# Denominators in 32-row column tiles, reciprocals spread by DMA, moments from the add, and a fixed order table, in a linear-attention and gMLP kernel

## The chip, the cores and the metric

One core of one Trainium2 chip. The metric is the time in device microseconds (us) of one execution; a median of several executions is quoted, with the lowest and the highest in brackets. Nearly all runs here count as fast; the four single ones that were marked slow (one each of e1, e8, e9 and of the kernel before) are left out of every ratio.

## The reference, cut to what matters

```python
# x [1,2048,512]; 32 heads of 16; F half = 896
q, k, v = split(layernorm(x) @ wqkv)
pq, pk  = phi(q), phi(k)                  # phi(t) = (t+1 if t>0 else exp(t)) + 1e-6
kv  = einsum('bhsd,bhse->bhde', pk, v);  z = pk.sum(over s)
num = pq @ kv;   den = einsum('bhqd,bhd->bhq', pq, z) + 1e-6    # one number per token and head
h   = x + (num / den) @ wo
z   = gelu(layernorm(h) @ w_in);  z1, z2 = halves of z;  z2 = layernorm(z2)
g   = w_sp @ z2 + b_sp                    # "mixing": over the 2048 tokens
out = h + (z1 * g) @ w_out
```

The parts that matter: the division by `den`, the moments of `h` for the second layer norm, and the mixing, whose matrix `w_sp` (8 MB) must be brought in and transposed while the first half runs.

## The kernel before

Every operation is recorded with its engine, its reads and writes and a modelled cost; a scheduler then fixes one order for each of the five engines, and each engine works through its own order and never overtakes. Most instructions therefore carry a helper's line number, and one goes by the names of the tiles. The division works on whole 128-row tiles, with z spread by a mask into a 128x128 matrix, so that each denominator comes out on all 16 rows of its head:

```python
    for tg in range(NG):                       # 4 groups of 512 tokens
        for c in range(0, KD, 2):
            q, r = pqT[:, c:c + 2, tg * GW:(tg + 1) * GW], r16[len(dens) % 2]
            for i in (0, 1):
                matmuls(bank(DB + i), [(zmat[:, c + i, :], q[:, i, :])])
            act(r_t, pair(DB), ACT.Ln, 2 * GW, bias=epst[:, 0:1], extra=[epst])
            dens.append(act(r, r_t, ACT.Exp, 2 * GW, scale=-1.0))       # 1/den
            dve(lambda v, q=q, r=r: v.tensor_tensor(q, q, r, ALU.mult), ...)
    for n in range(NT):                        # 16 tiles of h
        matmuls(bank(b), [(pqT[:, c, n * P:(n + 1) * P], m[:, c, :]) for c in range(KD)])
        dve(... v.tensor_tensor(h[:, n, :], bank(b), x[:, n, :], ALU.add) ...)
        stats(h, 1, n)                         # BN stats and aggregate on DVE
        rstd(...); norm(...)                   # GpSimd, then DVE: hn
        g.last = dma_t(hnT[:, :, n * P:(n + 1) * P], hn, f"ht{n}")   # SyncE transposes
```

The loads of `w_sp` are 64 transposing DMAs on the same SyncE, 16 for each of four groups of 512 tokens. All 16 of one group raise one semaphore, so a reader of any tile of a group waits for the whole group. The scheduler does not model this: in its times a reader waits for the tiles that it reads.

```python
    order = [t for p in range(NG // 2) for tg in (p, p + NG // 2) for t in range(tg * TPG, (tg + 1) * TPG)]
    for t in order:                            # groups 0, 2, then 1, 3
        for j in range(0, NT, 4):
            dma_t(wsp[:, j:j + 4, t * P:(t + 1) * P], ..., f"wsp{t // TPG}").deps.add(...)
```

The mixing is done in two rounds, with a seven-product block scheme: groups 0 (`lo`) and 2 (`hi`) first, then 1 and 3. The sums of blocks of `w_sp` that it needs (t1, t2 and so on) are made by DVE:

```python
    for p in range(NG // 2):
        for tok, b in ((lo, EB[0]), (hi, EB[1])):
            matmuls(bank(b), [(z2[:, s, last * P:KF * P], wsp[:, s, tok]) for s in range(NT)])
            gate(last, tok, b, bsp[:, tok])    # DVE reads the bank: u, then z1T. Frees the bank
        op = combine(t1, y12, y11, ALU.subtract)       # y12, y11: half of the tiles of groups hi and lo
        combine(t2, y22, t1, ALU.subtract)
        ...
        for k in range(HF): cell(k, lo, hi)    # s1 @ t1 into bank EB[c], ...
```

Of the kernel before, what the change touches and what calls it, by code (L numbers as in the profile page):

```python
# [3 lines left out]

FP32 = mybir.dt.float32
# [7 lines left out]
LOOK = 160.0  # L13
ROUNDS = 1200
# [16 lines left out]
class _Prog:  # L31
# [110 lines left out]
    def _pass(self, rank, back):  # L142

        ops = self.ops
        pre = [o.users if back else o.deps | o.soft for o in ops]
        nxt = [o.deps | o.soft if back else o.users for o in ops]
        left = [len(p) for p in pre]
        ready = [0.0] * len(ops)
        free = {e: 0.0 for e in self.ENGS}
        cand = {e: [] for e in self.ENGS}  # L150
        for o in ops:
            if not left[o.i]:
                cand[o.eng].append(o.i)
        start = [0.0] * len(ops)
        for _ in ops:
            best = None
            for e in self.ENGS:
                c = cand[e]
                if not c:
                    continue  # L160
                t0 = max(free[e], min(ready[i] for i in c))
                pick = min((i for i in c if ready[i] <= t0 + LOOK), key=lambda i: (rank[i], i))
                t0 = max(t0, ready[pick])
                if best is None or t0 < best[0]:
                    best = (t0, e, pick)
            t0, e, i = best
            cand[e].remove(i)
            start[i] = t0
            free[e] = t0 + ops[i].cost
            for u in nxt[i]:  # L170
                lag = self._lag(ops[u], ops[i]) if back else self._lag(ops[i], ops[u])
                ready[u] = max(ready[u], free[e] + lag)
                left[u] -= 1
                if not left[u]:
                    cand[ops[u].eng].append(u)
        return start

    def _value(self, start):

        v = max(start[o.i] + o.cost + o.lat for o in self.ops)  # L180
        last = None
        for t, c in sorted((start[o.i], o.cost) for o in self.ops if o.eng == "PE"):
            if last is not None and t - last > 800:
                v += (t - last - 800) * 0.5
            last = t + c
        return v

    def _swing(self, rank, n):

        best = None  # L190
        for _ in range(n):
            start = self._pass(rank, False)
            v = self._value(start)
            if best is None or v < best[0]:
                best = (v, start)
            late = self._pass([-(start[o.i] + o.cost) for o in self.ops], True)
            rank = [-(late[o.i] + o.cost) for o in self.ops]
        return best

    def schedule(self):  # L200
        ops = self.ops
        for o in ops:
            for d in o.deps | o.soft:
                ops[d].users.append(o.i)
        for o in reversed(ops):
            o.prio = max((ops[u].prio + self._lag(o, ops[u]) for u in o.users), default=o.lat) + o.cost + o.bias
        best = self._swing([-o.prio for o in ops], 20)
        rng = np.random.default_rng(0)
        for _ in range(ROUNDS):
            t = np.array(best[1])  # L210
            a, w = rng.uniform(0, 0.6 * best[0]), rng.uniform(5e3, 4e4)
            if rng.random() < 0.4:
                a, w = 0.0, best[0]
            near = (t >= a) & (t < a + w)
            got = self._swing(list(t + near * rng.normal(0, rng.choice([200, 600, 1500, 3000]), len(ops))), 2)
            if got[0] <= best[0]:
                best = got
        self.est, self.start = best
        self.seq = sorted(ops, key=lambda o: (self.start[o.i], o.i))
        self.order = {e: [o for o in self.seq if o.eng == e] for e in self.ENGS}  # L220
# [91 lines left out]
def bass_sequential_preLN__linear_attn_block__mixer_gmlp__prompt_kernel(  # L312
# [92 lines left out]
    r_t = g.sbuf("r", o_r, [2, GW], FP32)  # L405
    r16 = [g.sbuf(f"r16{b}", o_ct + b * 2 * GW * 2, [2, GW], BF16) for b in range(2)]
# [4 lines left out]
    zmat = g.sbuf("zmat", o_z, [KD, P], BF16)  # L411
# [14 lines left out]
    sel = const("sel", [8], FP32)  # L426
    epst = const("epst", [8], FP32)
# [12 lines left out]
    def bank(b, n=512, lo=0):  # L440
        return psum[:, b, lo:lo + n]
# [68 lines left out]

    wq = A_wqkv.rearrange("(c p) f -> p c f", p=P)
# [25 lines left out]
    for n, t in ((8, 7600), (10, 8300), (12, 9100), (14, 9900)):  # L537
        load_x("SP", n, 2, t)
    first_load("SP", wqkv[:, :, 0:D], A_wqkv[:, 0:D], "wq", 11400)
    g.add("ACT", lambda ac: ac.preload_act_table_set("natural_log_exp_and_others"), [], [], cost=1300).soft.add(  # L540
        queue["ACT"][-1].i)
# [7 lines left out]
    def rstd(s, r, n, w, col, neg, sign=1.0):  # L549

        rr, ss = r[:, n:n + w, :], s[:, n:n + w, :]
        pool(lambda p: p.tensor_scalar(rr[:, :, 1:2], ss[:, :, col + 1:col + 2], sign, EPS_LN, op0=ALU.mult,  # L552
                                       op1=ALU.add), [ss[:, :, col + 1:col + 2]], [rr], 230)
        pool(lambda p: p.tensor_tensor(rr[:, :, 0:1], rr[:, :, 1:2],  # L554
                                       expo[:, 0:w].rearrange("p (a b) -> p a b", b=1), ALU.pow), [rr, expo], [rr],
             620 + 120 * (w - 1))
        if neg:
            for i in range(n, n + w):
                pool(lambda p, i=i: p.tensor_scalar(r[:, i, 2:3], s[:, i, col:col + 1], r[:, i, 0:1], -1.0,
                                                    op0=ALU.mult, op1=ALU.mult), [r[:, i, :], s[:, i, :]], [r[:, i, :]], 240)  # L560

# [24 lines left out]
    def phi(dst, b, w=2):  # L586

        e, t = e_t[ecnt[0] % NE][:, 0:w, :], psum[:, b:b + w, :]
        ecnt[0] += 1
        act(e, t, ACT.Exp, w * GW)  # L590
        dve(lambda v: v.tensor_scalar(e, e, 1.0, EPS_PHI, op0=ALU.min, op1=ALU.add), [e], [e], w * GW, acc=4)
        dve(lambda v: v.scalar_tensor_tensor(dst, t, 1.0 + EPS_PHI, e, op0=ALU.add, op1=ALU.max),  # L592
            [t, e], [dst], w * GW, ps=True)
# [60 lines left out]
    def z_unit():  # L654
# [20 lines left out]
        for c in range(KD):  # L675
            dve(lambda v, c=c: v.tensor_scalar(zmat[:, c, :], bmask, bank(zb + 1, 1, c), None, op0=ALU.mult),
                [bmask, bank(zb + 1)], [zmat[:, c, :]], P)

    QS = {8: 1, 10: 1, 12: 1, 14: 1}
# [33 lines left out]
    for c in range(KD):  # L713
        b = CB[1 - c % 2]
        matmuls(bank(b), [(kvm[:, c, :], wo[:, c, :])])
        if c % 2:
            act(m[:, c, :], bank(b), ACT.Copy, GW)
        else:
            dve(lambda v, c=c, b=b: v.tensor_copy(m[:, c, :], bank(b)), [bank(b)], [m[:, c, :]], GW, ps=True)
# [5 lines left out]
    DB, dens = 6, []  # L725
    for tg in range(NG):
        for c in range(0, KD, 2):
            q, r = pqT[:, c:c + 2, tg * GW:(tg + 1) * GW], r16[len(dens) % 2]
            for i in (0, 1):
                matmuls(bank(DB + i), [(zmat[:, c + i, :], q[:, i, :])])  # L730
            act(r_t, pair(DB), ACT.Ln, 2 * GW, bias=epst[:, 0:1], extra=[epst])
            dens.append(act(r, r_t, ACT.Exp, 2 * GW, scale=-1.0))
            dve(lambda v, q=q, r=r: v.tensor_tensor(q, q, r, ALU.mult), [q, r], [q], 2 * GW, acc=2)  # L733


    AB = [4, 5]
# [4 lines left out]
    for n in range(NT):  # L741
        b = AB[n % 2]
        matmuls(bank(b), [(pqT[:, c, n * P:(n + 1) * P], m[:, c, :]) for c in range(KD)])
        dve(lambda v, n=n, b=b: v.tensor_tensor(h[:, n, :], bank(b), x[:, n, :], ALU.add), [bank(b), x[:, n, :]],  # L744
            [h[:, n, :]], D, ps=True)
        stats(h, 1, n)
        rstd(st[1], rs[1], n, 1, 6, HN(n) != "DVE")
        hn = hn_t[n % NH]
        norm(HN(n), hn, h[:, n, :], st[1], rs[1], n, 6, D)
        g.last = dma_t(hnT[:, :, n * P:(n + 1) * P], hn, f"ht{n}")  # L750
        if n == 0:
            first = g.last
# [3 lines left out]
    table.deps |= {o.i for o in dens}  # L756
    for n in range(NT):
# [14 lines left out]
        if n % 2 == 0 and n < NT - 2:  # L772
            gl = act(z2[:, n, :], src, ACT.Gelu_apprx_tanh, FH, accum=s[:, 0:1])
            act(sq_t, z2[:, n, :], ACT.Square, FH, scale=FH ** -0.5, accum=s[:, 1:2])
            pool(lambda p, s=s: p.tensor_scalar(s[:, 12:13], s[:, 0:1], 1.0 / FH, None, op0=ALU.mult), [s], [s], 190)
            dve(lambda v, s=s: v.scalar_tensor_tensor(s[:, 13:14], s[:, 12:13], s[:, 12:13], s[:, 1:2], op0=ALU.mult,
                                                      op1=ALU.subtract), [s], [s], 60)
            rstd(st3, rs3, n, 1, 12, False, -1.0)
# [6 lines left out]
        gl.deps.add(table.i)  # L785
# [7 lines left out]
    for tg in range(NG):  # L793
        for fc in range(KF):
# [3 lines left out]
            act(z1T[:, fc, tg * GW:(tg + 1) * GW], bank(b), ACT.Gelu_apprx_tanh, GW).deps.add(table.i)  # L798
# [112 lines left out]
```

## Time and profile before

| | before |
|---|---|
| median of 3 runs | 238.44 us (238.12 to 238.98) |
| span of the profiled execution | 239.5 us |
| busy: TensorE, DVE, ScalarE, GpSimd | 96%, 68%, 39%, 17% |
| last tile of `w_sp` group 2 issued by SyncE (103.11 + 8 x 1.31) | about 113.6 us |
| first sum t1 on DVE | 117.2 us |
| first matmul that reads t1 | 134.3 us |

A timeline line gives start, length, engine, line, operation, tiles out<-in, and how many instructions are merged; a bracket at the end is idle time before it and who ended it. A page's busy rows are shares of the span, its digits tenths of a slice. Four lines of the timelines of before, of SyncE's queue and of DVE, will be needed later:

```profile
103.11 14.38 SPq L491 DMA_TRANSPOSE wsp<-in_B_w_sp_dram  x11
117.53 1.08 SPq L488 DMA_DIRECT2D bsp<-in_B_b_sp_dram  x1
```

```profile
116.20 1.08 DVE L565 TENSOR_SCALAR z<-z,st,rs 128x896 bf16<-128x896 bf16 x2
117.20 2.28 DVE L830 TENSOR_TENSOR t<-wsp 128x4096 bf16<-128x4096 bf16 x1
```

The reader sees that SyncE hands out the last tiles of group 2 in the first run of eleven (nine of it; the last two are of group 1), only then b_sp, and that t1 starts on DVE without a wait. There are 17 us from t1 to the matmul that reads it, and z1 matmuls lie in between.

One trap: the granted-clock row of before has a 7 in its second slice. There TensorE ran at half its clock for 3.4 us ("half clock" from here on), right behind a hole (idle time of TensorE) of 1.87 us in the head; that costs 1.7 us of progress. It comes in some executions only: the profiled one of before had it (mean clock 0.993, 241.22 us), most of its other runs had not (0.998 to 1.000). Traces are therefore compared from a point after the head, times by medians.

### The profile page before, as it was taken

The page shows a single profiled execution, that of the slowest core. Times are in us where ns is not written, and L with a number is a line of the kernel's source. Part 1 is how long each engine was busy: PE and PEld are TensorE (multiplying, and loading weights), DVE is VectorE, ACT ScalarE, POOL GpSimd, SP SyncE. Part 2 cuts the span into 40 slices and gives each one's busy share as a digit, 9 for nine tenths or more (in the row PEclk, how much of TensorE's full clock was granted, in tenths as well). Part 3 has the DMA queues.
Part 4 walks back from the last instruction along what each step waited for, and adds up shares of the span by engine and source line. Part 5 has one row for each costly group of instructions (what it writes and reads, how often), then busy time and mean ns, then how long its engine had stood idle before and what let it go on. Part 6 is the DMA issues. An engine that isn't in the chain of part 4 may idle for free.

```text
span 239.5 us, 3027 instructions
## 1 busy us (share of the span) xinstructions
PE 229.2 (96%) x1118; PEld 107.1 (45%) x1140; DVE 163.4 (68%) x303; ACT 93.1 (39%) x134; POOL 40.2 (17%) x113
## 2 busy tenths in 40 slices
PE   7689999999989999999999999999999999999994
PEld 7244444463334444444434444444444444444441
DVE  3798766579998999954985538929659454443634
ACT  2276943479996477688460210100101010000000
POOL 4442400000114564773210000000000000000000
PEclk9799999999999999999999999999999999999999
DMA  6904359944413446444584453430000000010223
GB/s 213 311 5 88 75 139 374 226 105 94 109 27 66 105 92 84 96 104 93 105 164 107 97 102 89 97 78 0 3 0 0 0 0 3 22 66 1 88 68 110
DMA packets 57727, 21.58 MB, mean 90 GB/s; under 512 B 49520, under 2 KB 57584, under 8 KB 57712
## 3 DMA queue, kind: packets, MB, share of 16 engines
q1 hardware_dynamic: 56880, 20.59, 36.5%
q10 hardware_dynamic: 832, 0.79, 1.0%
q8 instruction: 9, 0.15, 0.3%
q14 instruction: 6, 0.05, 0.1%
HBM read 7.47 MB, written 2.10 MB: 40 GB/s over the span
## 4 chain that ended last, share of the span: by engine, by line
PE 78%; DVE 10%; ACT 4%; DMA 4%; issue 1%; POOL 1%; SPq 0%; DVEq 0%
PE psum L458 65%; PE psum L641 6%; PE psum L763 4%; DVE st L546 3%; PE psum L766 3%; DMA x<-in_A_x_dram 2%; DVE h L744 2%; ACT r L477 2%; DVE hn L565 2%; DMA hnT<-hn 1%; ACT e L477 1%; DVE pqT L592 1%; POOL rs L554 1%; DVE st L781 1%; DVE pqT L733 0%
## 5 line engine op out<-in xcount | busy, mean ns | idle before, releaser
L458 PE MATMUL psum<-wsp,z 128*128 128x512 bf16 x205 | 47.0, 379 | 0.2
L458 PEld LDWEIGHTS psum<-wsp,z 128*128 128x128 bf16 x208 | 20.4, 98 | 24.4 <-ACT psum L477 0.2
L477 ACT ACTIVATE psum<-psum 128x512 f32<-128x512 f32 x12 | 7.0, 582 | 61.8 <-PE psum L458 37.0
L458 PE MATMUL psum<-hnT,win 128*128 128x512 bf16 x110 | 26.4, 379 | 0.1
L554 POOL TENSOR_TENSOR rs<-rs,expo 128x1 f32<-128x1 f32 (+1 forms) x41 | 25.1, 614 | 3.1
L458 PE MATMUL psum<-wout,z1T 128*128 128x512 bf16 x109 | 25.0, 379 | 0.1
L458 PE MATMUL psum<-t,s 128*128 128x512 bf16 x95 | 22.5, 379 | 0.1
L477 ACT ACTIVATE z1T<-psum 128x512 bf16<-128x512 f32 x28 | 16.6, 595 | 14.8 <-PE psum L458 14.8
L477 ACT ACTIVATE e<-psum 128x1024 bf16<-128x1024 f32 (+1 forms) x18 | 16.7, 928 | 14.3 <-PE psum L458 14.2
L552 POOL TENSOR_SCALAR rs<-st 128x1 f32<-128x1 f32 (+1 forms) x41 | 9.1, 222 | 74.0 <-DVE st L547 63.0
L477 ACT ACTIVATE z<-psum 128x896 bf16<-128x896 f32 x16 | 14.6, 914 | 10.5 <-PE psum L766 10.4
L458 PE MATMUL psum<-wqkv,xnT 128*128 128x512 bf16 x61 | 16.7, 407 | 1.1 <-ACT xnT L477 0.7
L825 DVE TENSOR_TENSOR u<-psum,bsp 128x512 bf16<-128x512 f32 x16 | 10.9, 689 | 9.9 <-PE psum L458 9.7
L816 DVE TENSOR_TENSOR h<-psum,h 128x512 bf16<-128x512 f32 x16 | 10.5, 686 | 9.8 <-PE psum L458 9.8
L458 PEld LDWEIGHTS psum<-wout,z1T 128*128 128x128 bf16 x112 | 10.9, 98 | 13.3 <-DVE h L816 0.4
L763 PE MATMUL psum<-win,hnT 128*128 128x512 bf16 x60 | 15.9, 379 | 0.6 <-DMA hnT<-hn 0.5
L825 DVE TENSOR_TENSOR u<-psum,p 128x512 bf16<-128x512 f32 x12 | 8.2, 689 | 11.9 <-PE psum L458 11.9
L458 PEld LDWEIGHTS psum<-hnT,win 128*128 128x128 bf16 x112 | 10.5, 98 | 12.8 <-ACT z1T L477 1.9
L641 PE MATMUL psum<-pk,xn 128*128 128x512 bf16 x63 | 16.1, 379 | 0.1
L458 PE MATMUL psum<-m,pqT 128*128 128x512 bf16 x62 | 15.3, 380 | 0.6 <-DVE pqT L733 0.2
L458 PE MATMUL psum<-xnT,wqkv 128*128 128x512 bf16 x63 | 15.7, 379 | 0.1
L458 PEld LDWEIGHTS psum<-t,s 128*128 128x128 bf16 x96 | 9.4, 98 | 11.3 <-ACT psum L477 0.2
(81 smaller groups left out, 304.2 us busy)
## 6 DMA issues: line engine op xcount, KB each, us to landing
out_dram<-h SPq DMA_DIRECT2D x16, 128.0 KB, 1.7
win<-in_B_w_in_dram SPq DMA_DIRECT2D x2, 896.0 KB, 9.8
x<-in_A_x_dram SPq DMA_DIRECT2D x5, 256.0 KB, 6.8
wqkv<-in_A_wqkv_dram SPq DMA_DIRECT2D x2, 512.0 KB, 6.2
wsp<-in_B_w_sp_dram SPq DMA_TRANSPOSE x64, 2.8
wout<-in_B_w_out_dram SPq DMA_DIRECT2D x1, 896.0 KB, 9.3
wo<-in_A_wo_dram SPq DMA_DIRECT2D x1, 512.0 KB, 5.3
bsp<-in_B_b_sp_dram SPq DMA_DIRECT2D x1, 512.0 KB, 5.2
```

Source lines behind the costliest of these rows:

```text
L458: inst = pe.matmul(out_ap, lhsT=a, rhs=b, start=start and i == 0, stop=stop and i == len(pairs) - 1, **kw)
L477: return g.add("ACT", lambda ac: ac.activation(out_ap, in_ap, func, **kw), [in_ap, *extra], [out_ap] + ([accum] if accum is not None else []),
L546: dve(lambda v: v.bn_stats(s[:, 0:6], src[:, n, :]), [src[:, n, :]], [s[:, 0:6]], D)
L552: pool(lambda p: p.tensor_scalar(rr[:, :, 1:2], ss[:, :, col + 1:col + 2], sign, EPS_LN, op0=ALU.mult, op1=ALU.add), [ss[:, :, col + 1:col ...
L554: pool(lambda p: p.tensor_tensor(rr[:, :, 0:1], rr[:, :, 1:2], expo[:, 0:w].rearrange("p (a b) -> p a b", b=1), ALU.pow), [rr, expo], [rr] ...
L565: return dve(lambda v: v.tensor_scalar(dst, src, mean, rst, op0=ALU.subtract, op1=ALU.mult), [src, mean, rst], [dst], w + 460, acc=4)
L641: inst = pe.matmul(bank(CB[c]), lhsT=xn[:, i, c * P:(c + 1) * P], rhs=pk[:, i, :], start=i == 0, stop=i == NT - 1)
L744: dve(lambda v, n=n, b=b: v.tensor_tensor(h[:, n, :], bank(b), x[:, n, :], ALU.add), [bank(b), x[:, n, :]], [h[:, n, :]], D, ps=True)
L763: pe.matmul(bank(b), lhsT=hnT[:, c, n * P:(n + 1) * P], rhs=win2[:, c, 0:GW], start=c == 0, stop=c == KD - 1)
L766: inst = pe.matmul(bank(b + 1, F2), lhsT=hnT[:, c, n * P:(n + 1) * P], rhs=win2[:, c, GW:FH], start=c == 0, stop=c == KD - 1)
L816: dve(lambda v: v.tensor_tensor(o, bank(b), h[:, n, :], ALU.add), [bank(b), h[:, n, :]], [o], D, ps=True)
L825: dve(lambda v: v.tensor_tensor(t, bank(b), add, ALU.add), [bank(b), add], [t], GW, ps=True)
```

## The change

Three intents. (1) `den` is one number per head and token, so 32 rows hold it (4 copies of 8 heads) where 128 were computed; four such 32-row products sit side by side in TensorE, and Ln and Exp run on one bank in place of four. The price: each reciprocal must be spread from 32 rows to 128 by a DMA. (2) The moments of h come from an accumulator of the add and from a ScalarE square, and not from BN stats on DVE. (3) The order, which a randomised search found at build time, is now a stored table.

```diff
-    def _pass(self, rank, back): ...          # list scheduler, 1200 random restarts
+    def schedule(self):
+        ids = np.frombuffer(zlib.decompress(base64.b85decode(ORDER)), np.uint16).tolist()
+        ...                                    # the table is the order; only checked against deps
-    zmat = g.sbuf("zmat", o_z, [KD, P], BF16)
+    zc = g.sbuf("zc", o_z, [KD, 32], BF16)
@@ denominators
+    def spread(tg, c):
+        src, dst = rc[tg % 2][32 * c:32 * (c + 1), :], r16[tg][:, c, :]
+        src_ap = bass.AP(src.tensor, src.offset, [list(src.ap[0]), [0, 4], [1, GW]])
+        g.add("SP", lambda q: q.dma_start(dst, src_ap), [rc[tg % 2]], [dst], cost=480, lat=2500, ...)
     for tg in range(NG):
-        for c in range(0, KD, 2):
-            for i in (0, 1):
-                matmuls(bank(DB + i), [(zmat[:, c + i, :], q[:, i, :])])
-            act(r_t, pair(DB), ACT.Ln, 2 * GW, ...)
-            dens.append(act(r, r_t, ACT.Exp, 2 * GW, scale=-1.0))
+            for c in range(KD):
+                inst = pe.matmul(psum[32 * c:32 * (c + 1), db, :], lhsT=zc[:, c, :], rhs=pqT[:, c, tok], ...)
+        act_exp(r_t, bank(db), ACT.Ln, GW, ...)
+        act_exp(rc[tg % 2], r_t, ACT.Exp, GW, scale=-1.0)
+        for c in range(KD):
+            spread(tg, c)
@@ h
-    AB = [4, 5]
+    AB = [4, 5, 7]
-        dve(... v.tensor_tensor(h[:, n, :], bank(b), x[:, n, :], ALU.add) ...)
-        stats(h, 1, n)
-        rstd(st[1], rs[1], n, 1, 6, HN(n) != "DVE")
+        dve(... v.scalar_tensor_tensor(h[:, n, :], bank(b), 1.0, x[:, n, :], op0=ALU.mult, op1=ALU.add,
+                                       accum_out=s[:, 0:1]) ...)
+        act(sh_t[n % 2], h[:, n, :], ACT.Square, D, scale=D ** -0.5, accum=s[:, 1:2])
+        moments(s, 6, D)                       # GpSimd
+        rpow(s[:, 7:8], rs[1][:, n, 0:1])
```

(Cut: buffers, the selection mask, the moments of z2 moved to GpSimd, all four casts of m put on ScalarE, two query units recorded earlier, dependencies made "order only" on the table load.) The loops that record the `w_sp` loads and the mixing are unchanged in the source. Their order is not: it is in the table.

## The prediction

> **What bounds the kernel now.** I read the page first, from the busy shares to the slices to the chain of work that ended last.
>
> ```profile
> span 239.5 us, 3027 instructions
> PE 229.2 (96%) x1118; PEld 107.1 (45%) x1140; DVE 163.4 (68%) x303; ACT 93.1 (39%) x134; POOL 40.2 (17%) x113
> PE   7689999999989999999999999999999999999994
> PEclk9799999999999999999999999999999999999999
> PE 78%; DVE 10%; ACT 4%; DMA 4%; issue 1%; POOL 1%; SPq 0%; DVEq 0%
> ```
>
> TensorE is busy in all slices but the first two or three and the last, at a full clock, and is 78% of the chain. So a microsecond taken from TensorE's work, or from a hole in it, is a microsecond of the span; work taken from another engine counts only where TensorE waits for it. Which stretches are these? The timeline of TensorE and the table by stretches:
>
> ```profile
> 45.16 1.05 PE L662 MATMUL psum<-pk,ones 128*32 128x512 bf16 x16
> 46.14 1.90 PE L641 MATMUL psum<-pk,xn 128*128 128x512 bf16 x8
> ...
> 63.80 1.04 PE L458 MATMUL psum<-m,pqT 128*128 128x512 bf16 x4 [0.21 <-DVE pqT L733]
> 64.67 0.59 PE L458 MATMUL psum<-pqT,zmat 128*128 128x512 bf16 x2
> 65.11 1.03 PE L458 MATMUL psum<-m,pqT 128*128 128x512 bf16 x4
> 66.71 0.60 PE L458 MATMUL psum<-pqT,zmat 128*128 128x512 bf16 x2 [0.58 <-ACT r L477]
> ```
>
> ```profile
> 57.00:71.50 14.50, 13.03 (x59) 5.38 (x60) 14.23 (x26) 13.97 (x15) 1.50 (x4) 1.00 0.35 75
> 71.50:83.00 11.50, 11.28 (x55) 5.04 (x54) 10.84 (x28) 6.80 (x9) 5.51 (x14) 1.00 0.38 80
> 83.00:114.50 31.50, 31.34 (x157) 15.41 (x158) 24.84 (x67) 24.07 (x44) 18.79 (x50) 1.00 0.51 96
> ```
>
> (columns: stretch, length, busy PE, PEld, DVE, ACT, POOL, clock, DMA share, GB/s). From 57 to 71.5 us DVE and ACT are both full (14.23 and 13.97 of 14.50) and TensorE is not; this is where the denominators, their Ln and Exp, the multiplications by the reciprocals and the h tiles lie together. After 83 TensorE has no hole to speak of. I size the holes by counting. A 512-column matmul is issued every 0.216 us (32 of them from 124.80 to 131.71), a 384-column one every 0.163. Between the first query matmul at 48.90 and the first mixing matmul at 114.44 lie 32 query, 16 denominator, 4 kvm, 64 h, 64 z2 and 60 z1 matmuls of 512 columns (240 x 0.216 = 51.8), 64 of 384 columns (10.4) and the 16 small ones on ct (0.9): 63.1 us of work in 65.5 us. The holes are 2.4 us. From 114.44 to 236.4 are 564 matmuls, 121.8 us of work: no hole. The rest is the head (steady from 13.4 us) and a tail of 3.1 us (last h add and store).
>
> **What the Trainium skill says.** "TensorEngine Tiling (Array Packing)", Tiling Modes and Key Properties: 128 rows by 32 columns gives four tiles that run side by side, and a change of mode drains TensorE. The trace agrees: 16 matmuls of 32 columns took from about 45.06 (end of the four before) to 46.14, which is four times 0.216 and some 0.1 us of seam on either side. "DMA: Bandwidth & Descriptors", HWDGE ordering: each DMA engine consumes a queue's descriptors in ring order. So a small copy can queue behind the transposes that SyncE issued before it; no line of this trace isolates that. "VectorE: DVE Perf Modes", Two Vector instructions with no wait between them: an op that also writes its accumulator is two instructions. The trace of before has that on ScalarE only (an accumulator read of 0.19 us). The same page's perf-mode table: tensor_tensor on PSUM runs at one element a cycle, which agrees with 0.68 us for the 512-column h add.
>
> **The change, part by part.**
>
> ```profile
> L477 ACT ACTIVATE r<-psum,epst x8: 1104/1113/1142, 50.2 to 70.1; 128x1024 f32<-128x1024 f32 x8
> L477 ACT ACTIVATE r<-r x8: 1056/1057/1100, 51.4 to 71.3; 128x1024 bf16<-128x1024 f32 x8
> L733 DVE TENSOR_TENSOR pqT<-pqT,r x8: 658/682/686, 53.0 to 75.3; 128x1024 bf16<-128x1024 bf16 x8
> ```
>
> *Denominators on TensorE.* Removed: 16 x 0.216 = 3.46 us. Added: four sets of four 32-row tiles, each 0.216 plus two seams of 0.1 = 0.42, so 1.67. All on the path: **-1.8 us**.
>
> *Denominators on ScalarE.* Removed: 8 x (1.11 + 1.06) = 17.4. Added: 4 Ln and 4 Exp of 512 columns, about 0.6 each, 5; two more copies of m, 1.1. The 16 squares of h bring 16 x 0.63 = 10 (an 896-column square with its accumulator read advances the engine by 0.95; 384 columns less is 0.32 less). ScalarE ends level over the whole, but it is emptier by some 5 us before 66, when the reciprocals are wanted, and busier from 66 to 90, where it had holes.
>
> *Moments of h.* DVE loses 16 BN stats at a 0.60 pitch and 16 aggregates at 0.09, about 11 us, two casts of m (1.2) and the larger part of zmat (0.4). It gets 16 accumulator outputs in the h add, about 0.1 each (estimate, the model being ScalarE's). Net -10 or -11 us, most of it in 58 to 93 us, the stretch where DVE was full. The price is latency: h to normalised h was stats 0.6, aggregate 0.1, two GpSimd steps (0.28 and 0.6); it becomes a square (0.65), four GpSimd steps (3 x 0.28 and 0.6). That is 0.6 us longer for a tile with nothing in its way. But the first h tile of before was written at 58.3 and normalised only at 66.0, because DVE had no time for it, so I expect it earlier, near 62.
>
> *The spread by DMA.* 16 copies of 128 KB on SyncE, between its transposes.
>
> ```profile
> 0.79 0.40 SPq L488 DMA_DIRECT2D x<-in_A_x_dram  x1
> ...
> 43.38 21.47 SPq L491 DMA_TRANSPOSE wsp<-in_B_w_sp_dram  x16
> 66.43 8.26 SPq L491 DMA_TRANSPOSE hnT<-hn  x3
> ```
>
> A load of the same 128 rows of 1 KB took 0.40 us to issue, a store of 128 KB landed in 1.7 us; so 0.4 to 0.5 us of issue and 2 to 2.5 us to landing, with a transpose (1.3 us of issue) in front of some. SyncE is never the path while its work is 16 x 0.5 = 8 us longer, if the w_sp tiles still come in time. I walked its new order: with w_sp tiles at 1.30 us each and a long wait for the first reciprocals (about 43 to 51.5 us), the last tile of the first two groups lands near 121.5 us. The new TensorE order does all z1 before the mixing and starts it with tiles of the first group alone, so the second is wanted only some 10 us after the start: hidden.
>
> *The holes after the change.* I walked the new order of the five engines from 49 us with the durations above. First hole: the h tiles must wait for the second half of the first group's multiplication. Exp done at 51.6, four copies issued to 53.6, landed at 55.1 to 55.7, multiplied by 56.9, where TensorE has been free since 56.6: 0.3 us. Second: h tile 4 needs the second group's last copy, which stands behind three transposes, is issued at 59.0 and lands at 61; DVE multiplies by 63.1, TensorE is there at 62.5: 0.6 us. The later groups' copies land before DVE comes to them, and three banks for h (in place of two) cover its lag. About 0.1 more in small ones: 1.0 us where 2.4 were, **-1.4 us**.
>
> *Head and tail.* The first 15 us keep their order up to the second pair of tiles; the new selection mask is made in GpSimd's idle time; the tail is one add and one store as before. 0.
>
> Sum: -1.8 - 1.4 = -3.2. From 238.4 that is **235.2 us**, 1.4% less.
>
> **Rivals.** (a) *Only the count of matmuls is earned, the holes come back as waits for the spread.* For it: the reciprocal now goes through a DMA, so that a group is ready some 5 us after its matmuls instead of some 3, and the last copy of group 2 stands behind transposes. A landing time of 3.5 us instead of 2 adds about 1 us to each of the two holes. It gives 236 to 237.5. Against: the q units between fill most of it. (b) *The drained DVE gives everything back*: no holes, earlier first transposes of h; 233.8. For it: DVE at 98% in the stretch with holes. Against: TensorE cannot take z2 before hnT lands, and I see two waits that a lighter DVE does not cure. (c) *SyncE becomes the bound*: if a spread costs 0.8 us of issue, the 16 add 13 us to its queue; h transposes then come 3 to 5 us late and the mixing too: 238 to 240. Against: 0.40 for the like load. (d) *ScalarE delays z1 or z2 from 66 to 90* with squares ahead of the evictions: 10 us of squares in a stretch where ScalarE was 40% idle; up to 1 us.
>
> **Range and chances.** The matmul saving is nearly sure (1.5 to 2.4, by the seams). The holes may end anywhere between 0.2 and 3.5. So 233.6 to 237.2 holds it 8 times in 10. Faster by 2% means under 233.7, which wants every hole gone and a little more from head or tail: 0.14. Slower by 2% needs (c) at its worst: 0.02. Within 2%: 0.84.
>
> **What would show it.** Right: matmuls on zc in four groups of some 0.4 us each; TensorE busy 1.5 to 2 us less; mixing starts near 122 with all z1 done; DVE about 10 us less busy; first normalised h near 62 us; waits of TensorE for the multiplied pqT of 0.3 to 1 us. Wrong: TensorE waiting over 2 us for reciprocals or for hnT; w_sp named at the start of the mixing; spread copies with over 3 us to landing or over 0.7 us of issue; the squares in front of evictions that TensorE waits for; a gain in the head or the mixing that I have put at zero.

## The result, and the profile after

The changed kernel took **245.01 us** (243.98 to 246.83, 4 runs) against 238.71 us (238.12 to 239.13) for the kernel before in the same rounds: a ratio of **1.0274**, 95% interval 1.0207 to 1.0341. It is slower. A ratio is the mean time of one kernel's fast runs over that of the other's of the same rounds, so it isn't quite the ratio of the medians.

The page of after, the lines that answer to the first ones of before:

```profile
span 243.0 us, 3104 instructions
PE 229.3 (94%) x1140; PEld 105.6 (43%) x1140; DVE 150.1 (62%) x278; ACT 92.9 (38%) x160; POOL 55.1 (23%) x155
PE   7799999999969999999999579999999999999994
PEclk9999999999999999999999979999999999999999
PE 61%; SPq 20%; DVE 7%; DMA 5%; POOL 2%; issue 2%; ACT 2%; DVEq 0%
```

DVE is 13 us less busy, but the chain that ended last now spends 20% of the span in SyncE's queue, where it had 0%. TensorE's row has two dents, a 6 in the twelfth slice and a 5 in the twenty-third (about 134 to 140 us), and just behind the second the clock has a 7. (TensorE's busy totals can't be compared: the trace of before lacks 22 of 1140 matmul records.) The table of TensorE's waits in after names both dents (us in total, times, longest):

```profile
PE psum L401 <- DVE u L806: 4.2, 1, 4.2
PE psum L746 <- DMA hnT<-hn: 2.1, 2, 1.9
```

and the timeline of TensorE in after places them:

```profile
54.70 2.76 PE L401 MATMUL psum<-m,pqT 128*128 128x512 bf16 x12 [0.27 <-DVE pqT L713]
57.91 0.40 PE L703 MATMUL psum<-pqT,zc 128*32 128x512 bf16 x4 [0.45 <-DVE pqT L559]
61.31 3.63 PE L401 MATMUL psum<-m,pqT 128*128 128x512 bf16 x16 [0.31 <-DVE pqT L713]
69.04 1.04 PE L746 MATMUL psum<-win,hnT 128*128 128x512 bf16 x4 [1.92 <-DMA hnT<-hn]
...
123.19 13.97 PE L401 MATMUL psum<-wsp,z 128*128 128x512 bf16 x64 [0.20 <-DMA wsp<-in_B_w_sp_dram]
141.38 8.77 PE L401 MATMUL psum<-t,s 128*128 128x512 bf16 x32 [4.22 <-DVE u L806]
```

**Where the time went, by stretch.** Up to the mixing nothing is won or lost. From TensorE's first steady matmul on the second pair of tiles (13.43 us before, 11.00 after, both behind any half clock of the head) to the mixing with all z1 done (after: 123.19; before: 114.44 plus the 52 z1 matmuls still open there at 0.216, 125.67) it took 112.24 us before and 112.19 after. The matmuls saved 1.8 us, and the holes grew by as much. In the mixing the loss is 4.2 us of hole, and then 1.7 us: 32 matmuls took 8.77 us where 32 take 7.07. The table by stretches of after (length, busy time of the engines, then clock, DMA share, GB/s) shows why:

```profile
123.20:141.00 17.80, 13.97 (x64) 6.16 (x64) 12.89 (x19) 1.16 (x2) 2.39 (x4) 1.00 0.57 126
141.00:165.00 24.00, 23.62 (x102) 10.43 (x103) 16.51 (x25) 2.74 (x5) 0.00 (x0) 0.93 0.47 100
```

The clock of 0.93 over 24 us is 1.7 us lost: one window of 3.4 us at half rate; the clock records of the trace give it 3.413 us, from 142.35 on. The Trainium skill, "TensorE: Matmul & The Clock Gate", Part 1: The HAM clock gate, describes a free-running window of 3413 ns, and a clock that is halved after an idle one. The trace agrees on the length. 4.2 and 1.7 are 5.9 of the 6.3 us between the medians; the other 0.4 I don't account for.

**What the gate waited for.** The view of the chain that ended last, in order of time, between 124 and 141 us of after (start, length, what):

```profile
124.28 1.27 SPq L434
125.55 0.04 issue
125.60 0.58 SPq L431
126.18 0.05 issue
126.23 1.22 SPq L434
...
128.79 1.27 SPq L434
130.06 0.04 issue
130.10 2.90 DMA wsp<-in_B_w_sp_dram
...
133.10 2.29 DVE t L811
...
137.92 2.20 DVE t L811
```

SyncE issues one transpose after the other (1.27 each), then b_sp (L431), three more, and the fourth, issued at 130.10, lands 2.90 us later. Only then does t1 start. DVE's timeline of after shows what stands behind t1 in its fixed order:

```profile
127.68 0.68 DVE L811 TENSOR_TENSOR z<-z 128x1024 bf16<-128x1024 bf16 x1
133.10 2.29 DVE L811 TENSOR_TENSOR t<-wsp 128x4096 bf16<-128x4096 bf16 x1 [4.74 <-DMA wsp<-in_B_w_sp_dram]
...
137.84 2.28 DVE L811 TENSOR_TENSOR t<-wsp,t 128x4096 bf16<-128x4096 bf16 x1
...
140.64 0.68 DVE L806 TENSOR_TENSOR u<-psum,bsp 128x512 bf16<-128x512 f32 x1
```

The gate u at 140.64 frees the bank that the t·s matmuls want, and it stands behind t1, four small sums, t2 and another small one. So a DMA that is 4.7 us late becomes a TensorE hole of 4.2. "DVE u" is the name in the table of waits, but DVE had sat idle for 4.74 us of it.

Which DMA? The table puts three tiles of group 1, three of group 3 and b_sp ahead of the last tile of group 2, which is thus the 38th of the 64 tiles and not the 32nd. But t1 does not read that tile. It reads eight of the group's 16, and by the table the last of these eight is the 34th tile, issued at 124.28, just ahead of b_sp. The view of the tile wsp in after, for the issues of the 33rd and 34th tile, says how long they took to land:

```profile
L434 SPq DMA_TRANSPOSE wsp<-in_B_w_sp_dram x2: 1267/1267/1267, 123.0 to 124.3; - x2
DMA to landing us min/median/max: 2.7/2.8/2.9
```

So all that t1 reads had landed by 127.2, and DVE came to t1 at 128.36. It then waited until 133 for tiles of the other half, only because the 16 tiles share one semaphore. The model behind the table leaves this out: in its times t1 starts at 124.4, the last tile lands at 128.3 and is first read by t2 at 129.1, and the gate has about 0.4 us to spare. When the table is replayed with the same costs but with each reader waiting for its whole group, t1 starts 4.0 us later and a hole of 3.6 us opens at the gate; with the tiles sorted by group (e1 below) the replay loses nothing. (These replays are worked out from kernel.py and were not run on the chip.) On the chip SyncE was also about 4.7 us behind the model by the end of the h transposes (99.82 against 95.08), but TensorE came to the mixing 4.1 us behind it too (123.19 against 119.13), so this lateness explains little of the hole. One known part of it is the issue of a copy: 15 of the 16 took 0.59 to 0.67 us and one 1.94, where the model has 0.48. From the timeline of SyncE in after, and the table of DMA issues of after (KB each, median us to landing):

```profile
62.43 3.89 SPq L694 DMA_DIRECT2D r<-rc  x4
66.36 2.60 SPq L434 DMA_TRANSPOSE hnT<-hn  x2
```

```profile
r<-rc SPq DMA_DIRECT2D x16, 128.0 KB, 2.7
```

The first of these lines also explains the other dent: the second h transpose was issued behind four spread copies, at 66.36, and TensorE waited for it until 69.04. One of these four is the copy of 1.94 us; in e1 and e7 one of the same four took 1.68 and 1.62. Why is not known.

### The profile page after: what moved, and what is told of

The parts are those of the page before. It is cut to its first block, busy times and chain, and to the rows that moved or that the text cites. A ratio compares the mean times of both kernels' runs of the same rounds, so it can differ in the third digit from the quotient of the medians.

```text
span 243.0 us, 3104 instructions
## 1 busy us (share of the span) xinstructions
PE 229.3 (94%) x1140; PEld 105.6 (43%) x1140; DVE 150.1 (62%) x278; ACT 92.9 (38%) x160; POOL 55.1 (23%) x155
## 4 chain that ended last, share of the span: by engine, by line
PE 61%; SPq 20%; DVE 7%; DMA 5%; POOL 2%; issue 2%; ACT 2%; DVEq 0%
PE psum L401 52%; SPq L434 17%; PE psum L608 6%; DMA x<-in_A_x_dram 2%; SPq L694 2%; DVE t L811 2%; DMA wsp<-in_B_w_sp_dram 1%; DMA r<-rc 1%; DMA hnT<-hn 1%; DVE st L502 1%; POOL rs L527 1%; ACT sh L420 1%; PE psum L746 1%; DVE h L725 1%; DVE s L811 1%
## 5 line engine op out<-in xcount | busy, mean ns | idle before, releaser
L401 PE MATMUL psum<-wsp,z 128*128 128x512 bf16 x208 | 46.5, 379 | 0.2 <-DMA wsp<-in_B_w_sp_dram 0.2
L401 PE MATMUL psum<-t,s 128*128 128x512 bf16 x96 | 23.4, 400 | 4.2 <-DVE u L806 4.2
L401 PE MATMUL psum<-hnT,win 128*128 128x512 bf16 x112 | 25.6, 379 | 0.0
L762 DVE BATCH_NORM_STATS2 st<-z 128x6 f32<-128x512 bf16 x9 | 6.2, 689 | 16.9 <-ACT z L420 16.9
L521 POOL TENSOR_SCALAR st<-st 128x1 f32<-128x1 f32 x23 | 5.4, 237 | 48.4 <-ACT sh L420 34.3
L401 PEld LDWEIGHTS psum<-hnT,win 128*128 128x128 bf16 x112 | 9.8, 97 | 13.6 <-ACT z1T L420 4.4
L401 PE MATMUL psum<-wqkv,xnT 128*128 128x512 bf16 x64 | 15.1, 379 | 0.3 <-ACT xnT L420 0.3
L401 PE MATMUL psum<-m,pqT 128*128 128x512 bf16 x64 | 14.8, 379 | 0.6 <-DVE pqT L713 0.6
L608 PE MATMUL psum<-pk,xn 128*128 128x512 bf16 x64 | 15.1, 379 | 0.0
L527 POOL TENSOR_TENSOR rs<-st,expo 128x1 f32<-128x1 f32 x23 | 13.7, 598 | 1.1
```

Of the source, the lines that this page charges most:

```text
L401: inst = pe.matmul(out_ap, lhsT=a, rhs=b, start=start and i == 0, stop=stop and i == len(pairs) - 1, **kw)
L521: pool(lambda p: p.tensor_scalar(mean, s[:, 0:1], 1.0 / n, None, op0=ALU.mult), [s[:, 0:1]], [mean], 190)
L527: pool(lambda p: p.tensor_tensor(r, ve, expo[:, 0:1], ALU.pow), [ve, expo], [r], 620)
L608: inst = pe.matmul(bank(CB[c]), lhsT=xn[:, i, c * P:(c + 1) * P], rhs=pk[:, i, :], start=i == 0, stop=i == NT - 1)
L762: dve(lambda v, n=n, s=s: v.bn_stats(s[:, 0:6], z2[:, n, 0:GW]), [z2[:, n, 0:GW]], [s[:, 0:6]], GW)
```

## The experiments

**The theory** (Theory A in the expectations; other letters there are each run's own): the loss is the place of the last group-2 tiles in SyncE's order. **Rivals:** DVE's order (the gate behind t2) is the loss; the copies keep SyncE too long, whatever the order of `w_sp`; the parts of the change cost time by themselves. No run gives each half of a group a semaphore of its own, so that share of the mechanism rests on the landing times above, on e4 and on b1. All runs computed the right result.

### e1: the same 64 places, the tiles sorted by group

```diff
         assert len(ids) == len(self.ops)
+        at = [k for k, i in enumerate(ids) if str(self.ops[i].dma).startswith("wsp")]
+        by_group = sorted((ids[k] for k in at), key=lambda i: "0213".index(self.ops[i].dma[3]))
+        for k, i in zip(at, by_group): ids[k] = i
```

> The changed kernel with one edit: the 64 w_sp transposes keep their places in SyncE's order, but the groups come in the order 0, 2, 1, 3, so that the last tile of group 2 is the 32nd and no longer the 38th behind six tiles of groups 1 and 3 and the b_sp load. Theory A (late group-2 tiles hold t1 on DVE, the gate of the last column block stands behind t1 in DVE's order, and TensorE waits for its bank 4.2 us, which also drops its clock to half for 3.4 us): the last group-2 tile lands near 123, t1 starts at about 128.3 when DVE is through with z2, the gate ends near 136.5, the hole at 137 and the half clock are both gone, and the time is 245.0 - 4.2 - 1.7 = 239.1, give or take 0.8. Theory B (it is the mixing stage that suffers from having no z1 matmuls left to fill in, whatever the tiles do): the hole only shrinks, over 242. Theory C (the half clock has a cause of its own): hole gone, clock drop stays, 240.8.

Measured: **238.34 us** (237.10 to 240.87, 20 runs), ratio to before 0.9976 (0.9960 to 0.9992). The timelines of DVE and of TensorE in e1:

```profile
127.76 0.68 DVE L815 TENSOR_TENSOR z<-z 128x1024 bf16<-128x1024 bf16 x1
128.36 2.28 DVE L815 TENSOR_TENSOR t<-wsp 128x4096 bf16<-128x4096 bf16 x1
...
135.90 0.68 DVE L810 TENSOR_TENSOR u<-psum,bsp 128x512 bf16<-128x512 f32 x1
```

```profile
122.91 14.06 PE L405 MATMUL psum<-wsp,z 128*128 128x512 bf16 x64
136.81 7.07 PE L405 MATMUL psum<-t,s 128*128 128x512 bf16 x32
```

t1 starts 4.74 us earlier, exactly the wait it had; the hole and the half clock are gone (32 matmuls in 7.07). Nothing of the new arithmetic was touched. The order of the tiles is worth all of the loss. The gate's place in DVE's order is the same as in after, so that order costs nothing once the tile is in time.

### e2: the tile late as in after, but the gate ahead of the sums on DVE

```diff
+        k, late = ids.index(686), [690, 691, 688, 716, 717, 696, 719, 738]   # 686: the gate's multiplication
+        ids = [i for i in ids[:k + 1] if i not in late] + late + [i for i in ids[k + 1:] if i not in late]
```

> The changed kernel with one edit: SyncE's order is left, but on DVE the gate of the last column block (tokens of group 0) stands before t1, and t1 and t2 follow it at once. Theory A: the tiles still land at 133, but the bank is freed at about 134.5; t2 is ready near 139.2 and TensorE wants it at 138.9, so the hole is 0.3 to 0.8 instead of 4.2, there is no half clock, and the time is about 239.7. If the late landing alone were the cause (TensorE needs t1 itself, wherever the gate stands), the hole stays over 3 us and the time over 244.

Measured: **240.89 us** (240.14 to 242.69, 5 runs), ratio 1.0075 (1.0024 to 1.0126). Two thirds of the loss went, and the half clock with it. I had expected 239.7. The timeline of TensorE in e2 shows a hole of 0.43 us left for t2 itself, with 1.6 us of small waits for gates and copies nearby in the table of waits:

```profile
136.38 1.90 PE L403 MATMUL psum<-t,s 128*128 128x512 bf16 x8
138.71 5.35 PE L403 MATMUL psum<-t,s 128*128 128x512 bf16 x24 [0.43 <-DVE t L813]
```

So an order that asks for the late data last loses less, but the cure lies with the tile.

### e3: the spread copies issued by GpSimd

```diff
-        g.add("SP", lambda q: q.dma_start(dst, src_ap), [rc[tg % 2]], ...)
+        g.add("POOL", lambda q: q.dma_start(dst, src_ap), [rc[tg % 2]], ...)
```

> The changed kernel with one edit: the 16 spread copies are issued by GpSimd and not by SyncE. Theory A with its second half (the copies' 16 x 0.6 us on SyncE push the w_sp tiles and the second h transpose back): all of SyncE is some 8 to 10 us earlier after 60 us, group 2 has landed near 124, no hole at 137 and no wait of 2 us for the second h transpose near 67; 237 to 240, with the risk that the copies land later from GpSimd, or hold up the moments there, by 1 or 2 us. If SyncE's time is not what counts: 244 or more.

Measured: **253.47 us** (4 runs), ratio 1.0592: a miss. GpSimd works in order too. It waited once, 21.6 us long, for the reciprocals, and the moments of h stood behind that wait; the table of waits of e3 shows TensorE waiting for the multiplied pqT:

```profile
PE psum L401 <- DVE pqT L713: 9.0, 2, 7.0
```

It tells little about SyncE's time, since it moved the copies to a queue that had other things to do; t1's wait for `w_sp` was still 3.9 us with no copy on SyncE.

### e4 and e6: the new program under the scheduler of before

e4 replaces the table by one that the scheduler of before finds for the new program with the same costs; e6 is e4 with the sorting lines of e1.

> The changed kernel with another table: the one that the scheduler of the kernel before finds for exactly this program with its own list of durations. Theory A' (the loss sits in the table that was given and not in the new operations): 235 to 241, less than the given table by over 4 us. Theory D (the new parts themselves, the DMA spread and the longer way of the moments, cost the time): 244 or more.

> The program of after with the table made by the scheduler of before (which took 266.1 us, with one wait of 22.8 us for a w_sp tile of the first group), and now its w_sp tiles handed out group by group in the same places of SyncE's queue, first group first. Theory A (a scattered order of the w_sp tiles is the loss, in this table as in after's; the parts themselves are worth a little): the wait of 22.8 us is gone and the half clock after it; 239 us or less, 237 to 240. Rival B (the parts cost time whatever the order of w_sp: the spread copies keep SyncE too long): over 242.

Measured: e4 **266.08 us** (4 runs, ratio 1.1129), e6 **243.50 us** (242.28 to 244.47, ratio 1.0188, 1.0142 to 1.0234). e4 was expected at 235 to 241 and failed by the very mechanism under test, at the start of the mixing and for group 0 (timeline of TensorE in e4):

```profile
133.50 3.30 PE L401 MATMUL psum<-wsp,z 128*128 128x512 bf16 x8 [22.82 <-DMA wsp<-in_B_w_sp_dram]
```

That table issued the last tile of group 0 as the 39th of the 64. The eight matmuls that waited read eight tiles of the group, and these had landed by 63.2; here too the wait is for the shared semaphore. Sorting alone took 22.6 us off, so the theory holds in a second table. But e6 is over the 240 that it allowed, and in the range of the rival of that run (over 242). What is left there are many waits of 0.3 to 1.5 us from the head to the mixing, none for `w_sp`: for normalised x in the head (2.5 us in sum), for hnT (1.3), pqT (0.9 and 0.4), for ScalarE's evictions and for z2. A searched order of this program isn't good in itself, and e6 can't tell the share of the copies in it from that of the search.

### e7: SyncE's queue cleared in front of the h transposes

On top of e1:

```diff
+        off = [621, 635, 631]                  # w_sp tiles of group 0
+        ids = [i for i in ids if i not in off]
+        k = ids.index(316)                     # the fourth h transpose issued
+        ids[k + 1:k + 1] = off
```

(Tile 316 is the transpose of the third h tile, and the fourth to be issued.)

> The sorted kernel (238.3 us) with three w_sp tiles, which stood between the spread copies of the second and third group and the first h transposes, moved behind the third h transpose. They are needed only at 117 us. If SyncE's queue in front of the h transposes and copies is what makes the holes between 55 and 70 us (TensorE waited 1.5 us for hnT and 0.5 for pqT after the second group's last copy), both shrink below 0.5 together: 236.3 to 237.2. If the holes are set by DVE or by the landing time of the copies alone, no change: 238.3, and the waits stay above 1.5 in sum.

Measured: **240.34 us** (240.17 to 240.61, 4 runs), ratio 1.0074 (1.0059 to 1.0089), 2.0 us worse than e1. The timeline of TensorE in e7:

```profile
67.35 1.04 PE L754 MATMUL psum<-win,hnT 128*128 128x512 bf16 x4 [0.74 <-DMA hnT<-hn]
...
86.88 1.90 PE L409 MATMUL psum<-hnT,win 128*128 128x512 bf16 x8 [1.86 <-DMA hnT<-hn]
...
95.71 6.20 PE L409 MATMUL psum<-hnT,win 128*128 128x512 bf16 x28 [1.11 <-DMA hnT<-hn]
```

The holes that the edit aimed at shrank, from 1.51 to 0.74 us for hnT and from 0.51 to nothing for pqT; but later h transposes now stand behind the tiles that were moved, and two new holes of 1.86 and 1.11 us appear. SyncE's time between 60 and 100 us is spent in full: by reordering it can be passed around, not won. So SyncE's time isn't the 6 us; that the gain of the lighter engines went there fits with this run, but is not shown by it.

### e8 and e9: some copies on ScalarE

On top of e1, one copy of the second group goes ahead of the `w_sp` tile before it, so that three tiles follow it in a row, and two copies of the third group (e8), then two of the fourth as well (e9), are issued by ScalarE:

```diff
-        g.add("SP", lambda q: q.dma_start(dst, src_ap), ...)
+        g.add("ACT" if (tg, c // 2) in ((2, 1),) else "SP", lambda q: q.dma_start(dst, src_ap), ...)
+        for a, b in ((268, 266), (277, 251), (278, 277)):      # put a right behind b
+            ids.remove(a); ids.insert(ids.index(b) + 1, a)
```

> The sorted kernel (238.3 us), with one copy of the second group moved ahead of three w_sp tiles and two of the third group's four copies issued by ScalarE, which has just made the reciprocals, in place of SyncE. Moving w_sp tiles back only shifted the holes to 87 and 95 us (3.0 us of waits for hnT), so SyncE's queue is full from 60 to 100 us. If it is SyncE's issue time that makes the holes, taking 1.2 us off it, and off the way of the second h transpose, removes the waits of 0.5 us (multiplied pqT) and 1.5 us (hnT) and moves them nowhere: 236.3 to 237.3. If ScalarE's own issues (0.6 us each, in front of the squares of h) delay the h tiles as much, 238 to 238.8.

> As the kernel before it in this call, with two of the fourth group's copies on ScalarE too. SyncE is relieved by another 1.2 us, but ScalarE is nearly full there (4.55 of 5 us busy from 67 to 72 us), so its squares and evictions come 1.2 us later. The theory of SyncE's time gives no more than 0.3 us over the run with two; ScalarE being full would cost up to 1 us: 236.3 to 238.

Measured: e8 **237.91 us** (236.83 to 240.54, 22 runs), ratio to before 0.9965 (0.9948 to 0.9982); e9 **237.47 us** (237.19 to 242.45, 5 runs), ratio 0.9945 (0.9928 to 0.9961). e8 is outside its range of 236.3 to 237.3, though it goes the right way: the wait of 0.51 us for pqT is gone, but not the one of 1.5 us for hnT. The timeline of TensorE in e8:

```profile
66.81 1.04 PE L753 MATMUL psum<-win,hnT 128*128 128x512 bf16 x4 [1.53 <-DMA hnT<-hn]
...
122.11 14.06 PE L408 MATMUL psum<-wsp,z 128*128 128x512 bf16 x64
```

It is another wait, though: for the first h transpose to land, and no more for the second. It was issued at 61.49 as in e1 (61.48) and landed 5.3 us later, where in e1 it was there by 65.93. With the copy moved ahead, three `w_sp` tiles stand in a row before it; that these delayed it is not shown. The mixing starts at 122.11, 0.8 us earlier than in e1. So time on SyncE can be won with another issuing engine, a little at a time. e9's profile fell in an execution with half clocks, so I quote only its time. It has the lowest median, and is 0.55% under before; its interval overlaps with that of e8.

### e10: a dose of the cause

```diff
+        ids = [i for i in ids if i not in (669, 683)]          # two tiles of group 3
+        k = ids.index(643)                                     # the last tile of group 2
+        ids[k + 1:k + 1] = [669, 683]
```

> A dose of the theory: after, with only the two w_sp tiles of group 3 that stand ahead of the last tiles of group 2 moved behind them (the four tiles of group 1 and the load of b_sp stay ahead). The last tile of group 2 is issued 2.6 us earlier, so t1, t2 and the first gate end 2.6 us earlier and TensorE's wait before 141 us falls from 4.2 to about 1.6; with a hole so short there is no half clock, which took 1.7: 245.0 - 2.6 - 1.7 = 240.7, range 240.0 to 241.5. If the lateness of that tile is not the cause, 244 to 246 as before.

(The four tiles that stay ahead are three of group 1 and one of group 3; I had miscounted.)

Measured: **242.62 us** (241.49 to 243.77, 4 runs), ratio 1.0151 (1.0103 to 1.0200): between after and e1, but outside the range. DVE and TensorE in e10:

```profile
131.47 2.29 DVE L814 TENSOR_TENSOR t<-wsp 128x4096 bf16<-128x4096 bf16 x1 [3.41 <-DMA wsp<-in_B_w_sp_dram]
```

```profile
122.69 13.97 PE L404 MATMUL psum<-wsp,z 128*128 128x512 bf16 x63
139.75 8.64 PE L404 MATMUL psum<-t,s 128*128 128x512 bf16 x31 [3.10 <-DVE u L809]
```

t1 came 1.63 us earlier and not 2.6: the last two tiles of group 2, now right behind the 512 KB of b_sp, took 5.3 and 4.5 us to land, where the last one took 2.9 in after. The hole went from 4.22 to 3.10, and the half clock still came (in the trace at 139.52, before the hole ended), all in all in two of four executions (clock 0.993: 242.96 and 243.77; clock 1.000: 241.49 and 242.28). Without it, e1's 238.3 plus 3.1 is 241.4, near the mean of 241.9. The dose works with its measured size.

### b1: the same late tile in the kernel before

```diff
         self.seq = sorted(ops, key=lambda o: (self.start[o.i], o.i))
+        sp = [o for o in self.seq if o.eng == "SP"]
+        k = max(k for k, o in enumerate(sp) if o.dma == "wsp2")        # last tile of group 2
+        self.seq.remove(sp[k])
+        self.seq.insert(self.seq.index(sp[k + 7]) + 1, sp[k])          # behind 6 tiles and b_sp
```

> The reverse, in the kernel before: the last w_sp tile of group 2 moved behind seven later loads (six w_sp tiles of groups 1 and 3 and b_sp), as far as in after; nothing else. If a late tile of that group is enough for the loss whatever the other parts are: its landing goes from about 116.5 to 125 us, the sum t1 waits for it at the head of DVE's queue, the last normalised z2 tiles and the second block of the mixing come 6 to 7 us late, and with a half clock the run takes 244 to 247. If the kernel before has slack there (z1 matmuls stand between its first mixing blocks), 238.7 to 240, and after's order of TensorE shares the blame.

Measured: **249.23 us** (248.44 to 250.26, 4 runs), ratio 1.0435 (1.0401 to 1.0470). DVE and TensorE in b1:

```profile
123.70 2.29 DVE L835 TENSOR_TENSOR t<-wsp 128x4096 bf16<-128x4096 bf16 x1 [8.62 <-DMA wsp<-in_B_w_sp_dram]
```

```profile
130.29 8.80 PE L463 MATMUL psum<-wsp,z 128*128 128x512 bf16 x32 [7.53 <-DVE z L570]
```

None of the change's arithmetic is in this kernel, and one 128 KB tile in a late place costs it 10.4 us: 7.5 of hole and 1.7 of half clock behind it (32 matmuls in 8.80 us), which leaves 1.2 unplaced. The clock records of the profiled execution have two half-clock windows in a row, from 126.98 to 133.81; the first lies in the hole. The other executions (mean clock 0.979) had one more, which no trace places. Here the late t1 blocks the last normalisation of z2 in DVE's order, not the gate; the z1 matmuls between the blocks of the mixing did not help, because TensorE doesn't overtake either. A late tile of that group is enough. And t1 does not read the tile that was moved: it belongs to the half that t2 reads. That t1 nevertheless waited 8.62 us for it, and started when it had landed, shows the shared semaphore at work.

### p1 and p2: each part alone

On the program under the scheduler of before, with `w_sp` sorted: p1 keeps the 32-row denominators and the spread, with BN stats for h; p2 keeps the new h moments, with 128-row denominators.

```diff
 p1:  h loop and moments of h as in the kernel before; the rest as in after
 p2:  zmat, denominators, Ln and Exp as in the kernel before; the rest as in after
 both: search at build time as before, then the tiles of w_sp sorted by group
```

> One part alone: the 32-row denominators and the spread by DMA, with the h moments by BN stats on DVE as before; scheduled by the scheduler of before, w_sp in order. TensorE loses the 1.8 us that my sum gave to the matmuls; if that comes through, 236.6 against 238.4, and if the longer way of the reciprocals eats it, 238 to 239.5. TensorE's waits before 80 us decide which.

> The other part alone: the h moments from the h add and a ScalarE square, with the 128-row denominators of before; scheduled by the scheduler of before, w_sp in order. DVE is 10 us less busy. My sum gave the drained DVE 1.4 us of holes; if so, 237. If the holes are not DVE's, the same as before, 238.4, and if the squares delay ScalarE where the reciprocals are made, 239 to 240.

Measured: p1 **249.78 us** (249.28 to 251.17, 4 runs), ratio 1.0477 (1.0443 to 1.0511); p2 **242.96 us** (242.87 to 243.47, 4 runs), ratio 1.0187 (1.0171 to 1.0202). Both outside all their ranges. The search gave 235.3 and 236.0 us in its model, but for the order before the tiles were sorted; a replay of the sorted orders with the same costs gives 239.5 and 236.9. The chip is 10 and 6 us worse than that. Lines of TensorE in p1:

```profile
57.40 2.76 PE L464 MATMUL psum<-m,pqT 128*128 128x512 bf16 x12 [1.08 <-DVE pqT L776]
64.55 1.90 PE L464 MATMUL psum<-m,pqT 128*128 128x512 bf16 x8 [1.36 <-DVE pqT L776]
...
165.30 7.04 PE L464 MATMUL psum<-wsp,z 128*128 128x512 bf16 x24 [4.96 <-DMA wsp<-in_B_w_sp_dram]
```

p1 again lost 5 us to `w_sp`, now for the second round of the mixing (groups 1 and 3). Here the sorting lines did it: they put all of group 3 behind group 1, where the search had mixed the two, and the replay says that this costs 4.2 us even in the model; the two waits for pqT come where the reciprocals arrive by DMA and DVE is as busy as in the kernel before (162.5 us); I didn't take them apart. p2 has a wait of 1.14 us for the copies of m, which are all on ScalarE now. As a measure of what each part is worth the two runs are inconclusive, since each comes with another order. They do show that the model behind these tables is off by more than the parts are worth.

## Why the prediction was wrong

235.2 was predicted and 245.0 measured (3.2 of 238.4 is 1.3%, not the 1.4% that the text has). By its own steps:

* **TensorE bounds the kernel: right.** All of the loss that is accounted for is a hole in TensorE or its clock.
* **Denominators, -1.8 us: right.** The four groups on zc took 0.33 plus a seam of 0.09 at their start, 0.42 as worked out.
* **DVE 10 or 11 us less busy, the first normalised h near 62: right** in direction; 13 us less, and 59.3. The accumulator read is 0.08 us and lies beside the next instruction: h adds with it follow one another every 0.61 us.
* **Holes from 2.4 to 1.0 us, -1.4: wrong in sign.** Up to the mixing the holes took back the 1.8 us of the matmuls. The mis-sized terms: a copy issues in 0.59 to 0.67 us (one in 1.94), not 0.4 to 0.5, and lands in 2.7 (2.5 to 4.0), not 2 to 2.5; and the wait for the second h transpose, 1.92 us, is missing in the walk. The two holes that the walk gave as 0.3 and 0.6 measured 0.27 and 0.31. Rival (a) described this part.
* **"I walked its new order ... the last tile of the first two groups lands near 121.5 us ... the second is wanted only some 10 us after the start: hidden." This is the step that failed.** The tile landed at 133.05, 11.5 us later. I had counted tiles by kind and taken them to come in group order, as in the kernel before; the table mixes six tiles of groups 1 and 3 and b_sp in front. And "wanted 10 us after the start" named the matmuls that read the group and not t1, which waits for the whole group and stands on DVE in front of the gate that frees TensorE's bank. e1 (tile order), e2 (DVE order), e10 (dose) and b1 (the same in the kernel before) each show it.
* **Head and tail 0: not contradicted.** The two traces differ by 2.43 us in the head, where before's profiled execution had its half clock; that execution took 2.5 us more than the median of before's runs (241.22 against 238.71).
* **Not in the prediction at all:** the clock. A hole of 4.2 us cost 5.9.
* **Rival (c), SyncE becomes the bound, 238 to 240:** right in naming SyncE's queue, wrong in mechanism (h transposes and mixing late by the copies' issue time) and in size. Its chance of 0.02 for "slower" came from the copies alone, and the order of the 64 larger transposes beside them had none.

With the cause taken away (e1) the change gives 0.4 us by the medians, not 3.2: the 1.8 of the matmuls, less about 1.4 of new holes. e8 and e9, with some copies issued by ScalarE, have medians 0.4 and 0.9 us under e1's, so part of these holes is SyncE's issue time. **Open:** what a semaphore per half group would give; the worth of each part under an equally good order; the last 0.4 us of the loss; and why e6 stays at 243.5.

## What to carry to other kernels

A reordered list must be walked by the identity of what is moved, not by its kind: ask of each group which is its last member, where that stands, and which in-order queue behind its reader holds up TensorE. A scheduler must know every wait that the program really makes. Here a semaphore is shared by 16 loads and the model counted only the loads that are read, so it mixed the groups at no cost in its own times and at 6.7 us on the chip, which sorting won back (e1). Sorting is no cure in itself, as p1 shows: loads should come in the order in which their waits need them. And a hole in TensorE may bring a half clock behind it, already from about 1.9 us on in the traces here.

## What the Trainium skill lacked or had wrong

* "TensorE: Matmul & The Clock Gate", Part 1, gives half rate after at least one idle window of about 3.4 us. The length of the half-rate window agrees (3.413 us), but shorter holes were enough here: a half-clock window began in or within 1.3 us behind holes of 1.87 us (before), 2.17 (p2), 1.90 and 2.29 (e9) and 3.10 (e10). Holes of 1.92 (after), 1.95 (e3) and 1.86 us (e7) had none. (The ends of matmuls are modelled in the trace.) So no threshold follows from these runs, only a chance.
* "DMA: Bandwidth & Descriptors" has, as far as I found, no time measured on trn2 that SyncE needs to issue a transposing DMA or a copy with a repeated row. Here: 1.27 to 1.31 us for most transposes of 128 KB, 0.59 to 0.67 for 15 of 16 spread copies of 128 KB, 0.40 for the first plain load of that size. These times, not the transfers, filled SyncE's queue.
* The same page's HWDGE ordering speaks of descriptors in ring order. The runs add a size: two transposes right behind a load of 512 KB took 4.5 and 5.3 us to land in e10, and three took 3.4 to 4.3 in after, against a median of 2.9 over the whole run of after.
* "VectorE: DVE Perf Modes" says that an op which writes its accumulator is two instructions; the trace agrees. I found no time for the second: 0.08 us on DVE, hidden beside the next op (pitch 0.61), and 0.19 on ScalarE.
